# A new order of the first steps of a fused attention and MoE kernel, with a small first load and other engines for some steps

## The chip, the cores and the metric

The kernel runs on one core of one Trainium2 chip. The metric is the device time of one execution in microseconds. The core has five engines that run side by side and wait for each other by semaphores: TensorE (PE) multiplies matrices into PSUM, VectorE (DVE), ScalarE (ACT) and GpSimd (POOL) work on elements, SyncE (SP) issues the DMAs. Each engine executes its own queue strictly in order.

## The reference

Windowed attention with sink keys, and then an MLP with softplus on its result, all in float32, the weights given as float64 words (4 batches, 8 heads, 768 positions, head width 64; 3072 tokens, 512 to 2048 to 512).

```python
scores = scale * q @ k.T                      # per batch and head, scale = 1/8
rel = pos[:, None] - pos[None, :]
keep = (pos[None, :] < n_sink) | ((rel >= 0) & (rel < window))   # n_sink 4, window 128
scores = where(keep, scores, -1e9) - max
a = exp(scores); a = a / (sum(a) + 1e-09)
x = (a @ v) laid out as (tokens, 512)
h = x @ w_in
g = maximum(h, 0) + log1p(exp(-abs(h)))
out = g @ w_out
```

## The kernel before

**Tiling.** The 3072 tokens are cut into 12 chunks of 256. A chunk's attention has 8 heads, and its MLP has 8 slices s of 256 hidden columns. Matrices of the MLP are split into a high part that float32r holds exactly and a remainder, and three products are summed. Chunks 0 and 1 do their attention in plain float32, two heads at a time ("exact"); later chunks split the operands too. Step indices count heads through the chunks: 0 to 7 are chunk 0, 8 to 15 chunk 1, from 16 on chunk 2.

**Two orders.** The first steps stand in a string, `Ctx.START` (L1052), which `_fast` (L643) walks through: each letter calls a function, the number is its index. After it a loop runs the same pattern for every head until the end (`Ctx.STEADY`, L1048), and a tail follows. Since each engine works through its queue in order, what the string sets is the order within each engine's queue; what stands between on other engines doesn't matter. The letters are:

- S: scores of a head into PSUM (L249; from 16 on L266, L267). T: masks and softmax, on VectorE (L283 or L288, L295), and the exponential on ScalarE (L296). N: the sums (ScalarE, L309), the reciprocal (VectorE, L310), and the product on the engine that `Ctx.NM` names (L314 to L321; in exact chunks "A" means VectorE). W: transposes on TensorE (L357; from 16 on none), a copy on the engine of `Ctx.TH`, two selections on GpSimd (L362, L366). V: values (L422, L429; from 16 on L441, L447), into the one bank of tag x. O: high part on ScalarE and remainder xl on VectorE, which frees that bank. k and K: the sink weights (L326; transpose L337, copies on ScalarE, from 16 on subtractions on VectorE). In exact chunks only the odd index of a pair has work for N, W, V and O.
- w: the DMA of the next half weight. a, c, d, l: its four stages. a copies the top half words (engine from `Ctx.WT`), c joins them to the rest on VectorE (L519), into SBUF or, where `Ctx.WM` has p, into PSUM; d takes the high part (engine from `Ctx.WH`, P becoming A at home p), l the remainder (engine from `Ctx.WL`, always VectorE at home p). The halves come in the order wi00, wi01, wi10, wi11, wo00, wo01, wi20 and so on: wi is w_in, wo is w_out, then slice and half.
- U: up, 24 matmuls (L579). F: three activations of softplus on ScalarE (L586 to L588). P: gate, on VectorE (L594), and its high part gh on the engine of `Ctx.GH`. R: gl, the remainder (L609). D and E: the two halves of a down step, six matmuls each (L629), by row t; B: both halves joined, the four products with gh of each half first and the four with gl last.
- L, G: loads of q and k, and of v. p, q: splits of them. X, x: the transposes through DRAM from 16 on. J, j: the sinks' values on GpSimd. Z: dummy matmuls on a constant tile (L728).

**Masks.** `_constants` (L82) makes three masks from n_sink and window, which come in their own small DMA on ScalarE's queue (L91). A helper at L70 does every subtraction, one at L62, L64 and L66 every copy.

## Time and profile before

| | us |
|---|---|
| median of 3 runs | 685.43 (684.97 to 685.5) |
| the profiled execution, in all | 687.59 |
| its span, first to last instruction | 685.9 |
| TensorE busy in the span | 664.1 (97%) |
| VectorE busy | 523.3 (76%) |
| ScalarE busy | 473.3 (69%) |
| GpSimd busy | 432.4 (63%) |

Times in the trace are microseconds from the start of the span. A matmul's row shows its latency, and matmuls overlap, so rows can be longer than the distance between them. An idle time stands in brackets, with what ended it; that releaser is inferred, and of several it is the last one by the profile.

### The profile page before, as it was taken

How to read it: one execution, taken by the hardware profiler on the slowest of the kernel's cores; microseconds unless marked ns; L12 is line 12 of the kernel's file. 1: busy time of each engine (PE TensorE's matmuls, PEld its weight loads, DVE VectorE, ACT ScalarE, POOL GpSimd, SP SyncE). 2: the span in 40 equal slices, each digit the busy share in tenths (PEclk: the TensorE clock that was granted, in tenths of full speed). 3: DMA queues.
4: the chain of work that ended last, by engine and by line, in shares of the span. 5: the costliest groups of instructions: out<-in, count | busy, mean ns of one | idle time of the engine just before them, and what ended most of it. 6: DMA issues, size and time to landing. Idle time of an engine off the chain costs nothing. (4 is left out here: it accounts for less than half of the span.)

```text
span 685.9 us, 14212 instructions
## 1 busy us (share of the span) xinstructions
PE 664.1 (97%) x4319; PEld 595.3 (87%) x4319; DVE 523.3 (76%) x1461; ACT 473.3 (69%) x1213; POOL 432.4 (63%) x817
## 2 busy tenths in 40 slices
PE   5999889999999999999999999999999999999996
PEld 3588768999999999999999999999999999999985
DVE  6898987778888888887788788887978877754322
ACT  6998876767777677776777677776777677664322
POOL 6775458686676667677676775776766677653110
PEclk9999999999999999999999999999999999999999
DMA  8996334434434343543543544434434534310000
GB/s 304 353 403 207 95 77 126 103 103 131 107 94 139 102 116 112 130 115 83 148 102 98 134 113 113 124 103 108 131 94 119 143 91 118 104 52 0 32 5 32
DMA packets 97657, 83.35 MB, mean 122 GB/s; under 512 B 51876, under 2 KB 79140, under 8 KB 97572
## 3 DMA queue, kind: packets, MB, share of 16 engines
q1 hardware_dynamic: 97428, 82.35, 42.1%
q8 instruction: 37, 0.61, 0.4%
q14 instruction: 48, 0.39, 0.2%
q10 hardware_dynamic: 144, 0.00, 0.0%
HBM read 65.53 MB, written 16.78 MB: 120 GB/s over the span
## 5 line engine op out<-in xcount | busy, mean ns | idle before, releaser
L579 PE MATMUL h<-xh,wi 128*128 128x256 f32 x1536 | 247.3, 283 | 2.4 <-issue 1.5
L579 PEld LDWEIGHTS h<-xh,wi 128*128 128x128 f32 x1536 | 211.6, 191 | 7.5 <-issue 3.6
L629 PE MATMUL acc<-wo,gh 128*128 128x512 f32 x760 | 196.3, 394 | 1.2 <-POOL wo L70 1.2
L629 PEld LDWEIGHTS acc<-wo,gh 128*128 128x128 f32 x760 | 136.5, 188 | 26.0 <-POOL wo L70 1.5
L579 PE MATMUL h<-xl,wi 128*128 128x256 f32 x768 | 154.7, 283 | 0.0
L70 POOL TENSOR_TENSOR tl<-u,th 128x256 f32<-128x256 f32 x80 | 69.9, 874 | 133.0 <-issue 130.0
L579 PEld LDWEIGHTS h<-xl,wi 128*128 128x128 f32 x768 | 119.7, 192 | 0.0
L586 ACT ACTIVATE mt<-h 128x512 f32<-128x512 f32 x96 | 57.6, 600 | 88.3 <-PE h L579 76.0
L629 PE MATMUL acc<-wo,gl 128*128 128x512 f32 x380 | 106.6, 390 | 1.2 <-DVE gl L70 1.2
L66 POOL TENSOR_SCALAR gh<-mt 128x512 fp32r<-128x512 f32 x87 | 53.7, 618 | 73.1 <-DVE mt L594 36.7
L594 DVE SCALAR_TENSOR_TENSOR mt<-h,mt 128x512 f32<-128x512 f32 x96 | 63.3, 660 | 33.3 <-ACT mt L588 33.3
L629 PEld LDWEIGHTS acc<-wo,gl 128*128 128x128 f32 x380 | 71.3, 188 | 17.4 <-DVE gl L70 2.1
L296 ACT ACTIVATE a<-a,stats 128x136 f32<-128x136 f32 x192 | 76.5, 400 | 6.1 <-DVE stats L295 4.9
L70 DVE TENSOR_TENSOR gl<-mt,gh 128x512 fp32r<-128x512 f32 x95 | 72.3, 761 | 5.2 <-POOL gh L66 5.2
L62 ACT CAST qkh<-qk 128x656 fp32r<-128x656 f32 x80 | 59.0, 737 | 12.1 <-DMA qk<-qk 11.8
L321 POOL TENSOR_SCALAR a<-a,rc 128x128 f32<-128x128 f32 x156 | 63.8, 420 | 2.7 <-DVE rc L310 2.7
L70 DVE TENSOR_TENSOR qkh<-qk,qkh 64x256 fp32r<-64x256 f32 x80 | 40.8, 511 | 30.1 <-ACT qkh L62 28.7
L588 ACT ACTIVATE mt<-mt 128x512 f32<-128x512 f32 x96 | 60.7, 633 | 3.1
L587 ACT ACTIVATE mt<-mt 128x512 f32<-128x512 f32 x96 | 60.7, 633 | 3.1
L467 DVE TENSOR_TENSOR xt<-x,xt 64x256 f32<-64x256 f32 x80 | 33.0, 412 | 31.3 <-ACT xt L62 31.2
L70 DVE TENSOR_TENSOR kl<-qk,qkh 128x400 fp32r<-128x400 f32 x80 | 53.3, 667 | 2.3
L447 PE MATMUL x<-pt,vv 128*128 128x256 f32 (+1 forms) x216 | 47.3, 322 | 0.0
(195 smaller groups left out, 1103.1 us busy)
## 6 DMA issues: line engine op xcount, KB each, us to landing
qk<-qk SPq DMA_DIRECT2D x160, 164.0 KB, 3.1
rows<-xf SPq DMA_DIRECT2D x320, 32.0 KB, 1.6
u<-rows SPq DMA_DIRECT2D x80, 128.0 KB, 2.6
vr<-v SPq DMA_DIRECT2D x32, 192.0 KB, 2.7
out<-o SPq DMA_DIRECT2D x24, 256.0 KB, 2.4
qk<-qk SPq DMA_DIRECT2D x8, 328.0 KB, 6.6
vr<-v SPq DMA_DIRECT2D x16, 128.0 KB, 2.3
wi00r<-w SPq DMA_DIRECT2D x1, 511.8 KB, 6.6
```

What stands on the lines that cost most here:

```text
L62: nc.scalar.copy(out, in_)
L66: nc.gpsimd.tensor_scalar(out, in_, 1.0, 0.0, ALU.mult, ALU.add)
L70: (nc.vector if eng == "V" else nc.gpsimd).tensor_tensor(out, a, b, ALU.subtract)
L296: nc.scalar.activation(a, a, AF.Exp, bias=nm, scale=-1.0, accum_out=total)
L321: (nc.vector if eng == "V" else nc.gpsimd).tensor_scalar(a, a, rc[:, j : j + 1], 0.0, ALU.mult, ALU.add)
L447: nc.tensor.matmul(x[:, :, o], w, pt[:, :, m], start=False, stop=n == 2, skip_group_check=True)
L579: nc.tensor.matmul(h[:, j], wt, x, start=k == 0, stop=k >= len(prods) - 2, skip_group_check=True)
L586: nc.scalar.activation(t[:], h[:], AF.Abs)
L587: nc.scalar.activation(t[:], t[:], AF.Exp, scale=-1.0)
L588: nc.scalar.activation(t[:], t[:], AF.Ln, bias=1.0)
L594: nc.vector.scalar_tensor_tensor(t[:], h[:], 0.0, t[:], ALU.max, ALU.add)
L629: nc.tensor.matmul(self.acc[t][:], x[:, j, t * P : t * P + P], w, start=start, stop=stop, skip_group_check=True)
```

## The change

It leaves the computation as it is. n_sink and window, the first block of keys and the first queries of heads 0 and 1 come in one load of their own, `first`, ahead of the rest of those heads. All mask operations that the first softmax needs move to VectorE and ahead; those of masks 1 and 2 become a step m. A new step z runs dummy matmuls into the bank of tag x. gl gets its own list of engines, `Ctx.GL`, where it was always on VectorE. The lists of engines and `Ctx.START` are new: five of the first slices' down steps are joined (B0 to B3 and B6), and two more half weights have their home in PSUM.

```diff
@@ -87,8 +87,7 @@
 
 
     nc, cp = c.nc, c.const
-    words = cp.tile([P, 2, 2], I32, name="words")
-    nc.scalar.dma_start(words[:].rearrange("p a b -> p (a b)"), c.a["sizes"].broadcast_to([P, 4]))
+    words = c.first[:, :4].bitcast(I32).rearrange("p (a b) -> p a b", a=2)
     room = c.ap.tile([P, 1024], F32, tag="a", name="mask_room")
     used = 0
 
@@ -97,7 +96,7 @@
         used += n
         return room[:, used - n : used]
 
-    rel, key, lt, fold, first, r0, r1 = (scratch(n) for n in (P, NS, P, P, P, NS, NS))
+    rel, key, lt, fold, first, r0, r1, pen0, pen1 = (scratch(n) for n in (P, NS, P, P, P, NS, NS, NS, NS))
     nc.gpsimd.iota(rel, pattern=[[-1, P]], base=0, channel_multiplier=1, allow_small_or_imprecise_dtypes=True)
     nc.gpsimd.iota(key, pattern=[[1, NS]], base=0, channel_multiplier=0, allow_small_or_imprecise_dtypes=True)
     make_identity(nc, c.ident)
@@ -121,15 +120,18 @@
     nc.vector.scalar_tensor_tensor(sizes[:], top[:], 4294967296.0, words[:, :, 0], ALU.mult, ALU.add)
     c.ns, c.wd = sizes[:, 0:1], sizes[:, 1:2]
     m0, m1, m2 = c.masks = [cp.tile([P, KW], F32, name=f"mask{i}") for i in range(3)]
-    pen0, pen1 = scratch(NS), scratch(NS)
-    nc.gpsimd.tensor_scalar(pen0, r0, c.wd, -BIG, ALU.is_lt, ALU.mult)
     nc.vector.tensor_scalar(m2[:, P:], key, c.ns, -BIG, ALU.is_ge, ALU.mult)
+    nc.vector.tensor_scalar(pen0, r0, c.wd, -BIG, ALU.is_lt, ALU.mult)
+    nc.vector.tensor_tensor(m0[:, P:], m2[:, P:], pen0, ALU.min)
     nc.vector.tensor_scalar(m0[:, :P], first, c.wd, -BIG, ALU.is_ge, ALU.mult)
-    nc.gpsimd.tensor_scalar(pen1, r1, c.wd, -BIG, ALU.is_lt, ALU.mult)
-    nc.vector.tensor_tensor(m0[:, P:], m2[:, P:], pen0, ALU.min)
-    nc.vector.tensor_scalar(m1[:, :P], fold, c.wd, -BIG, ALU.is_ge, ALU.mult)
-    nc.vector.tensor_tensor(m1[:, P:], m2[:, P:], pen1, ALU.min)
-    nc.scalar.copy(m2[:, :P], m1[:, :P])
+
+    def later():
+        nc.vector.tensor_scalar(pen1, r1, c.wd, -BIG, ALU.is_lt, ALU.mult)
+        nc.vector.tensor_scalar(m1[:, :P], fold, c.wd, -BIG, ALU.is_ge, ALU.mult)
+        nc.vector.tensor_tensor(m1[:, P:], m2[:, P:], pen1, ALU.min)
+        nc.gpsimd.tensor_scalar(m2[:, :P], fold, c.wd, -BIG, ALU.is_ge, ALU.mult)
+
+    c.later_masks = later
 
 
 class _Attention:
@@ -195,7 +197,12 @@
         if self.exact:
             if h % 2 == 0:
                 r = c.lp.tile([P, QK], F32, tag=("qk", "qkh")[h // 2 % 2], name=f"qk{chunk}_{h}")
-                nc.sync.dma_start(r[:], c.a["qk0"][chunk, h // 2])
+                lo = 0
+                if chunk == h == 0:
+                    lo = KW
+                    c.first = c.stg.tile([P, 4 + KW + P], F32, tag="stg", name="first")
+                    nc.sync.dma_start(c.first[:], c.a["first"])
+                nc.sync.dma_start(r[:, lo:], c.a["qk0"][chunk, h // 2, :, lo:])
                 self.heads[h] = r
             return
         r = c.lp.tile([P, QK], F32, tag="qk", name=f"qk{chunk}_{h}")
@@ -245,8 +252,10 @@
         s = self.s[j] = pool.tile([P, 2, DM], F32, tag=tag, name=f"{tag}{chunk}_{h}_{j}")
         for e in range(2):
             rows = slice(e * D, e * D + D)
-            q = r[rows, KC + j * P : KC + j * P + P]
-            nc.tensor.matmul(s[:, e, :w], q, r[rows, j * KW : j * KW + w], start=True, stop=True)
+            q, k = r[rows, KC + j * P : KC + j * P + P], r[rows, j * KW : j * KW + w]
+            if chunk == h == j == 0:
+                q, k = c.first[rows, 4 + KW :], c.first[rows, 4 : 4 + KW]
+            nc.tensor.matmul(s[:, e, :w], q, k, start=True, stop=True)
 
     def scores(self, h):
         c, nc = self.c, self.c.nc
@@ -606,7 +615,7 @@
             gl = c.w[s, 0, 0][:, 1]
         else:
             gl = c.mp.tile([P, 2, CT], F32R, tag="gl", name=f"gl{chunk}_{s}", bufs=c.GB)[:]
-        _sub(nc, c.E["gl"], gl, t[:], self.g[s][0])
+        _sub(nc, _turn(c.GL, chunk * FP + s), gl, t[:], self.g[s][0])
         self.g[s].append(gl)
 
     def down(self, s, *js):
@@ -733,8 +742,17 @@
             out = c.idle[:, : 2 * P - NS]
             c.nc.tensor.matmul(out, c.sk[:, :P], c.sk[:, : 2 * P - NS], start=True, stop=True, skip_group_check=True)
 
+    def warm(k):
+
+        if c.warm is None:
+            c.warm = c.ps_x.tile([P, 2, CT], F32, tag="x", name="warm")
+        for _ in range(k):
+            out = c.warm[:, 0, : 2 * P - NS]
+            c.nc.tensor.matmul(out, c.sk[:, :P], c.sk[:, : 2 * P - NS], start=True, stop=True, skip_group_check=True)
+
     parts = {
         "Z": (idle, 0),
+        "z": (warm, 0),
         "S": (call(att, "scores"), G),
         "T": (call(att, "softmax"), G),
         "N": (call(att, "normalise"), G),
@@ -761,6 +779,7 @@
         "j": (sinks(1), G - 1),
         "Y": (next_sinks, 0),
         "w": (dma, 0),
+        "m": (lambda i: c.later_masks(), 0),
         **{kind: (stage(kind), 0) for kind in "acdl"},
     }
 
@@ -977,7 +996,7 @@
     nc = tc.nc
     c = Ctx()
     c.nc, c.tc, c.a, c.out = nc, tc, a, out
-    c.E = dict(qkh="A", ql="V", kl="V", vh="A", vl="P", xh="A", xl="P", gl="V", tl="P", out="AV")
+    c.E = dict(qkh="A", ql="V", kl="V", vh="A", vl="P", xh="A", xl="P", tl="P", out="AV")
     c.x, c.vs, c.vsr, c.vsh = {}, {}, {}, {}
     c.held_h, c.held_acc, c.tail = None, None, 0
     c.w64 = a["w"].dtype == mybir.dt.int64
@@ -1020,7 +1039,7 @@
             for n in ("ps_s", "ps_h"):
                 fronts[n] = st.enter_context(ExitStack())
             c.front_s, c.front_h = (scores_pool(f"front{n[2:]}", 1, own) for n, own in fronts.items())
-            c.follow, c.ps_s, c.ps_h, c.idle = follow, None, None, None
+            c.follow, c.ps_s, c.ps_h, c.idle, c.warm = follow, None, None, None, None
             c.xf = c.sp.tile([P, 2, CT], F32, name="xf", bufs=1)
             with tc.manual_schedule(engines=ORDERED):
                 m = _fast(c)
@@ -1037,29 +1056,30 @@
 
 Ctx.nchunks = B * NCH
 Ctx.GB, Ctx.EXACT = 3, 2
-Ctx.NM = "PPPPPAPPPAPAPPPVPAPPAPPPP"
-Ctx.TH = "VVVAAAAAAAVAAAVAAAAAAA"
-Ctx.GH = "PAAAAAVVVPPPP"
-Ctx.WM = "sssssssppsppssssssssssssssssssss"
-Ctx.WT = "AAVAAAAAAAAAAAAPPAAAAAAAAAAAAAAV"
-Ctx.WH = "APPPAAPAPPPPAAVAPAPAVAAVPAAAVAPA"
-Ctx.WL = "PPPVVPPVPPVVVPVPVPPVVVPPVPPVVPPV"
+Ctx.NM = "VPPPVAPPVVPVVVVPPAPPAPVPP"
+Ctx.TH = "AAAAAAAAAAVAVAAAAVAVVA"
+Ctx.GH = "AAPAPAPVPPAPP"
+Ctx.GL = "PVVVVVVPV"
+Ctx.WM = "sspspssppsppssssssssssssssssssss"
+Ctx.WT = "APAAAAAAAVAAAPPPPAAAAAAAAAPAAAAV"
+Ctx.WH = "APPPAAPPAPPAAPPPAAAAPAPPPAAPPVAA"
+Ctx.WL = "PPVPPPPPPVPPVPPPVVVVVVPVPPPPVPVP"
 Ctx.JOINED = 19
 Ctx.STEADY = (
     ("kWUqYpKSFTXRDVPONE", "SWTkpUKERDNFXPqYVO"),
     ("UKpFWSTRXPqNBVOYn", "WSpUKFTqBXVORPNnY"),
 )
 Ctx.START = """
-W0 N12 V14 V4 O4 V6 V0 S0 N6 V12 w j4 V2 N14 W14 O0 V10 N0 w w L8 O2 N2 S1 J0 w w w L10 L12 w T0 T1 S2 G4 w V8
-N1 w w w G8 w w G6 T2 L16 w w w w w G10 w L14 w w w w w w S3 T3 N3 w w w S4 T4 w W1 w k0 a a S5 T5 c c W12 w w
-L18 L17 G12 W8 d K0 d a S6 T6 c l l S7 W3 a O6 O8 S8 T7 d l O12 T8 c O14 d V1 N5 N7 O1 a a c d S9 T9 c N9 k4 a
-W5 V3 a Z4 S10 T10 l c c O3 Z18 S11 d K4 a a T11 l c N11 O10 l Z8 V5 O5 W7 S12 c a d d l l c d l d a c V7 O7
-N4 a k8 c l p16 d d a W9 U0 F0 U1 T12 c a a d P0 S13 T13 c R0 c d d K8 G14 N13 a F1 a U2 F2 l l l V9 S14 P1 l
-W11 W4 T14 G16 c l c W2 D0 a d S15 d P2 l L19 U3 a L20 T15 W13 R1 E0 c l S16 c N15 D1 O9 E1 k12 R2 E2 F3 d l d
-d a a T16 D2 P3 c a U4 L22 c l l a c d N16 R3 D3 d p17 c a p18 F4 d d V11 l l a K12 c d O11 a U5 N8 l l
-S17 F5 c T17 P4 c W10 l R4 p19 V13 O13 W15 X16 a a d S18 l a U6 E3 d T18 D4 P5 d c S19 T19 R5 l l d c p20 F6 q16 l
-l P6 N18 N17 J16 x16 E4 V15 X17 L21 G18 a O15 U7 x17 N19 S20 W16 c c c U8 D5 E5 F7 X18 k16 N10 T20 x18 R6 F8 P7 X19 R7 P8 K16 E6 d d d p21
-a D6 N20 W17 V16 W6 l l O16
+z3 w V10 N0 V0 j4 W0 W14 V12 w z6 N12 w N6 z4 w m J0 L8 G6 O0 V6 S0 w V14 L10 w w T0 L12 S1 T1 S2 G4 O4 w w V8 w
+L14 O8 V2 z1 N1 N2 O2 N14 w S3 T2 w V4 T3 L16 w N3 a w w z6 w w w S4 w w G8 a W1 W12 S5 w T4 k0 S6 w w O10 w w
+G10 w w c T5 w L17 c a z4 d O12 w w a K0 d T6 w l O6 c S7 w W8 S8 l G12 d T7 W3 T8 c l N5 N7 V1 O1 d a S9 a T9 c
+W5 S10 V3 c k4 N9 a S11 d a T10 l c c O3 d L18 K4 a T11 N4 l Z2 Z12 c O14 V5 a l O5 d W7 S12 c d d a l a l l d c
+c V7 O7 p16 l N11 d W9 W2 a U0 F0 k8 T12 c a d a c d a P0 U1 S13 T13 c K8 c d d R0 N13 l l F1 d U2 a l S14 F2
+G16 T14 l c l a W11 P1 c V9 L19 L20 l B0 a P2 a S15 T15 d W13 U3 R1 d G14 c c N15 a R2 O9 S16 l F3 k12 d c d W4
+B1 d a T16 P3 l l L22 a c c V11 B2 p17 l d d U4 R3 a c l N8 O11 l a d c F4 K12 a d N16 a l U5 F5 S17 T17 a l V13
+P4 c W10 c l d B3 O13 R4 p18 a W15 U6 p19 P5 d d S18 D4 E4 a S19 c l d T18 c T19 X16 R5 p20 l x16 F6 l l q16 l
+P6 N18 J16 N17 N10 V15 L21 G18 X17 D5 N19 U7 x17 E5 O15 a k16 c U8 c F7 W6 S20 X18 d R6 d W16 a P7 F8 c T20 x18
+B6 W17 P8 X19 K16 p21 N20 R7 V16 l d O16 l
 """
 
 
@@ -1074,6 +1094,12 @@
     w_out = w_out.reshape(FP, 2, P, DM).transpose(0, 2, 1, 3).reshape(FP, P, WC)
     w = np.stack([w_in, w_out], axis=1)
     return w.view(np.int64) if w.dtype == np.float64 else w
+
+
+def _first(qk, n_sink, window):
+    words = np.array([n_sink, window], np.int64).view(np.float32)
+    r = qk[0, 0, :2].reshape(P, QK)
+    return np.concatenate([np.broadcast_to(words, (P, 4)), r[:, :KW], r[:, KC : KC + P]], axis=1)
 
 
 def _layout(q, k, v, n_sink, window, moe_w_in, moe_w_out):
@@ -1093,7 +1119,7 @@
         "qk0": np.ascontiguousarray(qk[0, : Ctx.EXACT]).reshape(Ctx.EXACT, H // 2, P, QK),
         "v": np.ascontiguousarray(v.transpose(0, 2, 1, 3)).reshape(B, NB, P, H * D),
         "vs": np.ascontiguousarray(v[:, :, :NS].reshape(B, 2, G * NS, D).transpose(0, 2, 1, 3)),
-        "sizes": np.array([n_sink, window], np.int64).view(np.int32).reshape(1, 4),
+        "first": _first(qk, n_sink, window),
         "w": _blocks(moe_w_in, moe_w_out),
     }
 
```

## Rows read from the trace of the kernel before

**Rows 1.** Windows: us, then PE, PEld, DVE, ACT, POOL busy, PEclk, DMA, GB/s

```profile
30.00:40.00 10.00, 8.96 (x71) 7.09 (x70) 9.72 (x19) 9.68 (x22) 7.55 (x9) 1.00 1.04 342
...
300.00:400.00 100.00, 100.00 (x659) 91.88 (x658) 82.91 (x235) 72.28 (x190) 68.99 (x140) 1.00 0.43 115
```

**Rows 2.** Waits of TensorE, 0 to 200 us: total, times, longest

```profile
PE sb L249 <- DMA qk<-qk: 4.8, 1, 4.8
PE x L441 <- DVE sk L70: 2.4, 1, 2.4
PE acc L629 <- DVE gl L70: 1.2, 2, 0.8
...
PE s L266 <- DVE stats L295: 0.6, 1, 0.6
```

**Rows 3.** Timeline of TensorE: start, length, instruction, idle before and releaser

```profile
17.34 1.25 PE L249 MATMUL sb<-qk 64*128 64x264 f32 x4
...
21.15 0.77 PE L249 MATMUL sb<-qk 64*128 64x264 f32 x4
...
24.97 2.34 PE L734 MATMUL idle<-sk 128*128 128x248 f32 x18
...
35.31 0.72 PE L579 MATMUL h<-xh,wi 128*128 128x256 f32 x4
...
40.90 0.40 PE L579 MATMUL h<-xl,wi 128*128 128x256 f32 x2
...
72.54 0.67 PE L422 MATMUL x<-sk,vsf 128*128 128x256 f32 x2 [1.19 <-POOL wo L66]
```

**Rows 4.** Timeline of VectorE, single operations up to 101 us

```profile
5.29 0.16 DVE L120 SCALAR_TENSOR_TENSOR words_top<-words 128x2 f32<-128x2 int32 x1 [2.78 <-DMA words<-sizes]
...
6.75 0.30 DVE L295 CUSTOM_DVE_ANT_0 a<-sb,mask 128x136 f32<-128x136 f32 x1
...
15.29 0.45 DVE L64 CAST upper<-wi10r 128x512 f16<-128x512 bf16 x1
...
18.64 0.43 DVE L283 COPY_PREDICATED sb<-diag,sb 128x256 f32<-128x256 int32 x1 [0.99 <-PE sb L249]
...
31.89 0.69 DVE L314 TENSOR_TENSOR a<-a,rc 128x512 f32<-128x512 f32 x1
...
71.97 0.42 DVE L70 TENSOR_TENSOR xl<-x,xh 128x256 fp32r<-128x256 f32 x1 [0.22 <-ACT xh L62]
...
100.11 0.58 DVE L70 TENSOR_TENSOR sk<-ts,sk 32x128 fp32r<-32x128 f32 x2
```

**Rows 5.** Timeline of ScalarE: a top half, a high part, sink copies

```profile
13.15 0.76 ACT L62 CAST upper<-wi00r 128x512 f16<-128x512 bf16 x1
...
52.10 0.60 ACT L62 CAST wi<-wt 128x512 fp32r<-128x512 f32 x1
...
97.78 0.51 ACT L62 CAST sk<-ts 32x128 fp32r<-32x128 f32 x2
```

**Rows 6.** Timeline of VectorE beside GpSimd: stage c, and reads of a scores bank

```profile
27.90 0.68 DVE L519 SCALAR_TENSOR_TENSOR wt<-wi20r,upper 128x512 int32<-128x512 int32 x1
...
35.86 1.02 DVE L519 SCALAR_TENSOR_TENSOR word_ps<-wi31r,upper 128x512 int32<-128x512 int32 x1
...
58.59 0.48 DVE L288 COPY_PREDICATED s<-diag,s 128x128 f32<-128x128 int32 x2
...
60.89 1.78 DVE L519 SCALAR_TENSOR_TENSOR wt<-wo41r,upper 128x512 int32<-128x512 int32 x1
```

**Rows 7.** Timeline of GpSimd in the same stretches

```profile
36.29 1.06 POOL L66 TENSOR_SCALAR wo<-wt 128x512 fp32r<-128x512 f32 x1
...
58.00 1.84 POOL L70 TENSOR_TENSOR wo<-wt,wo 128x512 fp32r<-128x512 f32 x1 [0.94 <-ACT wo L62]
...
60.51 1.61 POOL L70 TENSOR_TENSOR wi<-wt,wi 128x512 fp32r<-128x512 f32 x1
```

**Rows 8.** DMA issues: KB, us from issue to landing

```profile
wi00r<-w SPq DMA_DIRECT2D x1, 511.8 KB, 6.6
```

## The prediction

> **What bounds the kernel now.** I first read the windows by stage. From about 110 us on TensorE is without a gap: 100.00 busy of 100 in the stretch from 300 to 400 us, beside 82.91 on VectorE and 72.28 on ScalarE [rows 1]. That part and the tail keep their order, so the change acts through the time at which the START list ends. TensorE's work in the list is the same in both orders (nine up steps, seven full down steps, the same scores, transposes and values); only its waits, its slow stretch and its dummy matmuls can go. Second, the waits of TensorE: 4.8 us before the first scores, 2.4 before the values V16, 1.2 in two waits for gl, 0.6 for a scores bank [rows 2]; and 1.19 before V13 [rows 3]. Third, the stage they arise in: between 30 and 40 us VectorE has 9.72 and ScalarE 9.68 of 10 us, GpSimd 7.55 [rows 1]. So up to U0 at 35.31 [rows 3] the elementwise queues are the bound, after it TensorE with them close behind, and in the end TensorE alone.
>
> V13's row names GpSimd's wo as its releaser. I read it otherwise: V13 needs the one bank of the x tag, which O11 frees, and O11's xl on VectorE ends at 71.97 + 0.42 = 72.39, 0.15 before V13 starts at 72.54 [rows 3, 4].
>
> Two up steps of 24 matmuls each take from 35.31 to 41.30 [rows 3]: about 2.9 for one, 0.12 for a matmul of 256 columns; so six of 512 columns, half a down step, take 1.4 (estimates).
>
> **Part 1, first DMA and masks.** From the words at 5.29 to the first softmax at 6.75 the masks take 1.46 us [rows 4]. All their operations stay on the path, since m stands ahead of T0 and puts mask 1 before it; only the turn to GpSimd goes, for two more eight-column VectorE operations. The words now come in the first of eight loads, which has 137 KB: no later than the 336 KB one that ends the wait of 4.8 [rows 2]. So T0 comes by 4.8 + 1.5 = 6.3 at the latest. I give that no credit of its own: the next long step on ScalarE is now the top half of wi00 (a), ahead of W1 and T4, and wi00 lands 6.6 us [rows 8] after its issue, which before was some 5.3 us in, so near 11.9; that step ran at 13.15 before [rows 5], behind T4. The split load puts one more issue and 67 KB ahead of wi00, 0.2 us at the 342 GB/s of [rows 1]. The early gain waits there for a weight.
>
> **Part 2, dummy matmuls.** The granted clock reads 1.00, the 2.4 GHz level, in both stretches of [rows 1], yet the same four scores matmuls take 1.25 us at 17.34 and 0.77 at 21.15 [rows 3]: early ones run slow. The new z steps put 13 matmuls ahead of S0 and 11 between S2 and K0. One costs 2.34 / 18 = 0.13 us [rows 3] at the fast rate, 0.21 at the ratio 1.25 / 0.77. The 13 take 1.7 to 2.7 us and run while TensorE waits for its first load; if that cover is too short they put S0 off by up to the excess, ahead of a ScalarE that waits for wi00. The 11 take 1.4 to 2.3 and are paid unless the pace rises, when each early scores step gives 0.5 back. What it can be worth is VectorE's wait of 0.99 for T8's scores [rows 4]. Z4 + Z18 + Z8 become Z2 + Z12, 2.1 us less, in a place where TensorE waits for O3 and W5 anyway: nothing.
>
> **Part 3, queues up to O7, so up to U0.** VectorE loses the top half of wi10 (0.45), Nm11 (0.69, now behind O7) and W1's copy (the same shape, 0.69), and gains one top half (0.45) [rows 4]: -1.4 us. ScalarE loses two top halves (0.76 each) and gains W1's copy and a high part (about 0.60 each) and one top half (0.76) [rows 5]: +0.4, less one short sum (Ns11) that moves behind O7. So U0 comes between no earlier (ScalarE is the bound) and 1.4 + 0.99 = 2.4 us earlier (VectorE is). Both are full, so I take the middle: **-1.2**.
>
> **Part 4, from U0 to V16.** By waiting step, from the order in the diff:
> - V13: between V11 and V13 stood K12, U5 and S17, some 3.4 us; now B2, U4, K12, U5 and S17, about 9. The wait of 1.2 goes.
> - gl: D needs gl at its third matmul, B at its ninth, some 1.4 us later. The waits of 1.2 in sum [rows 2] are at most 0.8 long: both go, unless gl itself is late. The two residues on GpSimd (R0, R7) stand where B0 and D7 have other steps ahead of them.
> - V16: now U8, S20, B6, K16, V16 in a row. B6 and S20 cover 3.3 us, under which F8, T20 and P8 run. Behind K16 nothing covers the sink copies: 0.51 on ScalarE [rows 5], 0.58 on VectorE [rows 4] and three handovers at 0.15, 1.55 in the place of 2.4: **-0.8**.
> - S19: between S18 and S19 there are D4 and E4, 2.8 us, where U6, E3 and D4 stood (5.7) and S19 still waited 0.6 [rows 2] for T18 to free its banks. Between T17 and T18 VectorE now has eight operations of the size of c (0.68 [rows 6]), two splits of about 1 and O13, 7.8 us, while TensorE has 7.7 (V13, B3, W15, U6). The wait lies between 0 and 3.5 (5.7 + 0.6 - 2.8), nearer to 0 because U6 has moved ahead of S18; I add **+1.2** for it and other new ones.
>
> Sum of the part: -1.2 - 1.2 - 0.8 + 1.2 = **-2.0**.
>
> **Part 5, work between engines.** Over START, counted from the lists (a weight with home p takes no GpSimd step): VectorE loses 3 high parts and 2 gh (about 0.45 each, as the cast of [rows 4]), 2 gl (as c, 0.68 each) and W1 (0.69), and gains a weight remainder (0.68) and W17 (about 0.35): -3.3 us. ScalarE loses 4 top halves (0.76 each), a high part and a gh (0.60 each): -4.2, with W1 and W17 about even. GpSimd gains 4 top halves, 4 high parts, 3 gh and 2 gl, less one remainder: eleven one-input operations of 0.5 to 1.06 [rows 7] and one of 1.61 [rows 7], 7 to 13 us, into a queue at 7.55 of 10. This makes the waits of part 4 less likely; it is not added again.
>
> What it costs lies on VectorE. Operation c is 0.68 alone and 1.78 beside a GpSimd remainder that runs from 60.51 to 62.12, and ends 0.55 after that [rows 6, 7]. Beside a one-input operation of GpSimd it took 1.02 [rows 6, 7], 0.34 more. But reads of a scores bank kept their time under the remainder from 58.00 to 59.84 [rows 7] (0.48 for two predicated copies at 58.59 [rows 6]). So one added GpSimd operation costs VectorE from nothing (beside reads of PSUM) to 0.34, or 1.1 with two inputs: 0 to 11 x 0.34 + 1.1 = 4.8 in all. I take 1.5, nearer to the lower end because half of VectorE's list reads PSUM; VectorE still gains, and the sum gets nothing.
>
> The Trainium skill, page "SBUF — State Buffer", section "Who interferes with whom", says that where the VectorE instruction has two SBUF inputs and the GpSimd one reads SBUF, the second to issue waits for the whole of the first. The trace agrees for c at 60.89, 1.1 us. By that rule one added one-input operation could cost up to all of its 0.5 or more, some 6.6 us for the twelve.
>
> **Sum.** -1.2 - 2.0 = **-3.2 us**. The profiled execution has a span of 685.90 inside 687.59 in all; its span would be 682.7. Against the median of the runs, 685.43: **682.2**.
>
> **Rivals.**
> - *The gain is given back at V16.* The last values need W16 on GpSimd. GpSimd's list there is l.wi71, q16, l.wo61, gh6, Nm18, J16, Nm19, W16, and S18 stands only some 17 us of TensorE work ahead of V16 (before: 21). If START ends when that chain does, V16's wait of 2.4 grows by what is won elsewhere. For it: GpSimd gets the added work. Against: it was idle a quarter of the time. It gives 685.2, no change.
> - *The pace doesn't rise early.* Then the 11 z steps put 2.3 us into TensorE's early queue; T8's wait grows by about 1.0 of them, and part 3's 1.2 isn't won: 682.2 + 1.2 + 1.0 = 684.4.
> - *GpSimd blocks VectorE (slower).* The place is U0 to T18, where VectorE is full. The added operations start first and c, kl and gl wait: 4.8 against 3.3 saved is 1.5 late, and the waits of part 4 stay, since their releasers (O11, T18, gl) sit on VectorE: 685.4 + 1.5 = 686.9. It decides from 3.3 us of added blocking: the two-input one and seven of the eleven. Against it is the row at 58.59 [rows 6].
>
> **How the numbers follow.** Forecast 0.60, given back 0.16, no early pace 0.08, blocked 0.16. The forecast's own range is 678.2 (2.4 at U0, 1.2 and 1.2 of waits, all 2.4 of V16, no new wait) to 684.5 (nothing at U0, 2.3 at S19). The whole range takes in the rivals, the last with a little over: 678.2 to 687.2. A difference of 0.2%, 1.4 us, is about what a measurement tells from none. Faster: 0.60 and half of the pace rival, 0.64; same: the other half and most of the given back, 0.19; slower: 0.17.
>
> **What would show it.** U0's first matmul near 34.1 instead of 35.31; no wait over 0.4 at V13 or for gl; V16 waiting about 1.6; scores of 0.77 rather than 1.25 well before 17 us; T0 before 6.3, but ScalarE waiting for wi00 near 11.9; c's mean not longer. The prediction is wrong if U0 stands at its old time, if S19 or U7 waits over 2 us, or if VectorE's two-input operations grow longer in sum.

## The result and the profile after

The changed kernel takes 691.42 us in the median (687.74 to 694.34), the kernel before 685.37 (684.97 to 685.84): 1.0082 times as long, 95% interval 1.0066 to 1.0098, or 6.05 us more. The prediction said 682.2. The profiled execution of the changed kernel took 692.79 us, with a span of 691.1.

The first part of its page (busy us, share of the span, instructions):

```profile
PE 667.7 (97%) x4327; PEld 601.3 (87%) x4327; DVE 525.7 (76%) x1461; ACT 469.5 (68%) x1205; POOL 444.9 (64%) x825
```

Its windows, to be held against [rows 1] (us; PE, PEld, DVE, ACT, POOL busy; PEclk; DMA; GB/s), and behind them two of the kernel before:

```profile
30.00:40.00 10.00, 9.48 (x76) 7.67 (x75) 9.53 (x15) 8.49 (x19) 6.93 (x9) 1.00 1.03 374
40.00:50.00 10.00, 8.61 (x56) 6.95 (x55) 9.60 (x28) 8.10 (x22) 8.12 (x9) 0.83 1.04 393
...
100.00:110.00 10.00, 7.27 (x36) 6.98 (x35) 8.25 (x23) 6.01 (x18) 9.71 (x15) 0.66 0.31 81
300.00:400.00 100.00, 100.00 (x661) 92.00 (x661) 81.93 (x234) 71.92 (x189) 69.36 (x139) 1.00 0.42 115
...
675.00:680.00 5.00, 4.74 (x23) 4.56 (x24) 0.69 (x1) 0.76 (x2) 0.35 (x1) 0.66 0.02 3
```

```profile
40.00:50.00 10.00, 9.61 (x70) 7.39 (x71) 9.90 (x29) 9.24 (x23) 6.01 (x7) 1.00 1.03 408
...
100.00:110.00 10.00, 7.97 (x51) 7.12 (x52) 7.17 (x21) 5.96 (x15) 7.01 (x12) 1.00 0.23 58
```

Between 300 and 400 us both kernels keep TensorE busy without a gap. What is new stands in PEclk: TensorE's granted clock is 0.83 in 40 to 50 us, 0.66 in 100 to 110 and 0.66 near the end, where the kernel before has 1.00. The waits of TensorE from 0 to 200 us, which answer to [rows 2] (total, times, longest):

```profile
PE x L450 <- ACT qkh L62: 2.7, 1, 2.7
...
PE sb L258 <- DMA qk<-qk: 1.5, 1, 1.5
...
PE s L275 <- DVE stats L304: 0.9, 1, 0.9
PE acc L638 <- DVE gl L70: 0.8, 1, 0.8
PE h L588 <- DVE mt L603: 0.8, 1, 0.8
...
PE s L276 <- DVE kl L70: 0.5, 1, 0.5
```

The wait of 4.8 for the first load has gone from this list, since the z matmuls now stand there; one wait for gl is left, and the wait before V16 is longer (2.7). TensorE's timeline, which answers to [rows 3]:

```profile
34.73 0.72 PE L588 MATMUL h<-xh,wi 128*128 128x256 f32 x4
...
43.06 0.74 PE L588 MATMUL h<-xh,wi 128*128 128x256 f32 x4 [0.77 <-DVE mt L603]
...
46.31 1.05 PE L588 MATMUL h<-xh,wi 128*128 128x256 f32 x4
...
102.89 0.55 PE L450 MATMUL x<-sk,vs 128*128 128x256 f32 x1 [2.73 <-ACT qkh L62]
...
104.09 1.05 PE L588 MATMUL h<-xh,wi 128*128 128x256 f32 x4
...
122.48 0.29 PE L275 MATMUL s<-qkh 128*128 128x264 f32 x1
...
671.99 0.71 PE L588 MATMUL h<-xh,wi 128*128 128x256 f32 x4 [1.07 <-PEq L1048]
...
675.26 1.06 PE L588 MATMUL h<-xh,wi 128*128 128x256 f32 x4 [2.32 <-issue]
```

U0 starts at 34.73. Behind the waits at 43.06 and 102.89 four matmuls of an up step take 1.05 us in place of 0.64, the half rate. The scores at 122.48 are the same step as at 119.24 in the first trace of the kernel before. Near the end TensorE waits twice, 3.4 us in sum: for its own sequencer (PEq), and for nothing that the profile names (issue). These two are called its own waits from here on.

**What a second trace of the kernel before shows (e15).** The execution on which the prediction rests took 687.59 us, 2.2 over its median. A second one took 685.43; from it first the waits, then the timeline of TensorE:

```profile
PE x L441 <- DVE sk L70: 2.0, 1, 2.0
PE acc L629 <- DVE gl L70: 1.3, 2, 0.9
PE acc L629 <- POOL wo L70: 1.2, 1, 1.2
```

```profile
70.95 0.60 PE L422 MATMUL x<-sk,vsf 128*128 128x256 f32 x2
...
117.09 0.29 PE L266 MATMUL s<-qkh 128*128 128x264 f32 x1
...
670.40 0.51 PE L579 MATMUL h<-xh,wi 128*128 128x256 f32 x3 [1.46 <-issue]
```

V13 starts at 70.95 without a wait, where [rows 3] has 1.19, and the scores come at 117.09. In the first execution a load of q and k was late. This row of ScalarE shows it, some 6 us ahead of V13; that it is what delayed V13 is likely, and was not tried:

```profile
66.14 0.74 ACT L62 CAST qkh<-qk 128x656 fp32r<-128x656 f32 x1 [1.99 <-DMA qk<-qk]
```

**The account, by the traces** (changed kernel against e15). START ends 122.48 - 117.09 = 5.4 us later. U0 comes 0.3 sooner (34.73 against 35.06). From U0 on the waits take 6.6 us against 5.3, so 1.3 more. The half rate costs 1.5 in U2 (4.56 us from its start to the next scores; 3.04 in e1, where the clock stays up) and 2.6 behind V16 (6.17 against 3.54 in e1). The last 0.3 stay unassigned. The loop from there to flag_row, the first matmul of the tail, is 0.9 shorter, and the tail 2.9 longer: its own waits 3.4 against 2.2, and half rate behind the second. The sum is 7.4 for these two executions, 692.79 against 685.43. The medians are 6.05 apart, so the traced execution of the changed kernel is 1.4 over its median, and the median need not hold each of these terms in full.

### The profile page after: what moved, and what is told of

It reads as the page before. It is cut to its first block, busy times and chain, and to the rows that moved or that the text cites. A ratio compares the mean times of both kernels' runs of the same rounds, so it can differ in the third digit from the quotient of the medians.

```text
span 691.1 us, 14220 instructions
## 1 busy us (share of the span) xinstructions
PE 667.7 (97%) x4327; PEld 601.3 (87%) x4327; DVE 525.7 (76%) x1461; ACT 469.5 (68%) x1205; POOL 444.9 (64%) x825
## 5 line engine op out<-in xcount | busy, mean ns | idle before, releaser
L588 PE MATMUL h<-xh,wi 128*128 128x256 f32 x1536 | 249.9, 285 | 4.2 <-issue 2.3
L588 PEld LDWEIGHTS h<-xh,wi 128*128 128x128 f32 x1536 | 214.8, 194 | 9.0 <-issue 4.0
L638 PE MATMUL acc<-wo,gh 128*128 128x512 f32 x760 | 193.3, 393 | 0.0
L588 PE MATMUL h<-xl,wi 128*128 128x256 f32 x768 | 156.4, 286 | 0.0
L588 PEld LDWEIGHTS h<-xl,wi 128*128 128x128 f32 x768 | 121.5, 195 | 0.0
L66 POOL TENSOR_SCALAR gh<-mt 128x512 fp32r<-128x512 f32 x89 | 56.6, 637 | 75.7 <-DVE mt L603 44.8
L638 PE MATMUL acc<-wo,gl 128*128 128x512 f32 x380 | 103.9, 390 | 0.8 <-DVE gl L70 0.8
L70 DVE TENSOR_TENSOR kl<-qk,qkh 128x400 fp32r<-128x400 f32 x80 | 55.1, 688 | 2.3
```

Of the source, the lines that this page charges most:

```text
L66: nc.gpsimd.tensor_scalar(out, in_, 1.0, 0.0, ALU.mult, ALU.add)
L70: (nc.vector if eng == "V" else nc.gpsimd).tensor_tensor(out, a, b, ALU.subtract)
L588: nc.tensor.matmul(h[:, j], wt, x, start=k == 0, stop=k >= len(prods) - 2, skip_group_check=True)
L638: nc.tensor.matmul(self.acc[t][:], x[:, j, t * P : t * P + P], w, start=start, stop=stop, skip_group_check=True)
```

## The experiments

Filler means: extra matmuls of a constant tile by itself into a tile of tag x, which nothing reads; one matmul is two records on TensorE. In the order they are a new letter y.

```diff
+    def plug(k):
+        t = c.ps_x.tile([P, 2, CT], F32, tag="x", name=f"plug{c.plugs}")
+        c.plugs += 1
+        for _ in range(k):
+            out = t[:, 0, :P]
+            c.nc.tensor.matmul(out, c.ident[:], c.ident[:], start=True, stop=True, skip_group_check=True)
```

All results in one table. "Records" is TensorE's count in the first part of the page; "tail at" is the start of flag_row, the first matmul behind the loop, in the traced execution; "own waits" are TensorE's waits for its sequencer and for issue near the end of that trace (in e18 the second, 1.8, is put down to ScalarE). The traced execution is one of several: it lies 2.4 us under the median in e6, 1.3 under it in e18 and 2.0 over it in e9 and e12.

| run | median us | ratio to before, 95% | records | tail at | own waits |
|---|---|---|---|---|---|
| before (first, second trace) | 685.3 to 685.6 | | 4319 | 657.07, 654.92 | 2.2, 2.2 |
| changed | 691.42 | 1.0066 to 1.0098 | 4327 | 659.42 | 3.4 |
| e1 late filler, 29 | 688.54 | 1.0036 to 1.0070 | 4385 | 658.80 | 0.9 |
| e2 without z | 690.82 | 1.0060 to 1.0094 | 4303 | 661.87 | 1.0 |
| e3 before without Z | 686.24 | 1.0002 to 1.0021 | 4289 | 657.38 | 1.2 |
| e4 before, new engines | 697.19 | 1.0155 to 1.0189 | 4319 | 666.87 | 2.1 |
| e5 late filler, 15 | 686.89 | 1.0012 to 1.0031 | 4357 | 658.74 | 0.9 |
| e6 K16 early | 690.99 | 1.0067 to 1.0101 | 4327 | 657.42 | 2.7 |
| e7 K16 early, filler 5 | 686.81 | 1.0012 to 1.0031 | 4337 | 657.23 | 0.9 |
| e8 before, first load and masks | 684.68 | 0.9979 to 0.9998 | 4319 | 654.52 | 1.5 |
| e9 e8 with K16 early | 685.65 | 0.9991 to 1.0011 | 4319 | 657.39 | 1.9 |
| e10 e8 with filler 8 | 683.22 | 0.9959 to 0.9984 | 4335 | 654.18 | 0.7 |
| e11 e7, less on GpSimd | 688.19 | 1.0031 to 1.0060 | 4337 | 658.84 | 1.1 |
| e12 e7, rows not joined | 686.95 | 1.0013 to 1.0035 | 4337 | 659.55 | 1.2 |
| e13 e5 with early filler | 687.09 | 1.0014 to 1.0034 | 4375 | 657.80 | 0.6 |
| e14 before, filler 8 | 684.19 | 0.9970 to 0.9989 | 4335 | 655.46 | 0.6 |
| e16 changed, filler 4 | 687.73 | 1.0020 to 1.0045 | 4335 | 659.00 | 1.2 |
| e17 changed, Z12 to Z4 | 688.48 | 1.0033 to 1.0067 | 4319 | 658.12 | 1.5 |
| e18 before, filler 4 | 687.87 | 1.0025 to 1.0054 | 4327 | 655.67 | 0.6 + 1.8 |

**Filling the waits behind which the clock falls (e1, e5, e13).**

```diff
-U1 S13 ... d U2 ... K16 p21
+U1 y5 S13 ... d y6 U2 ... K16 y18 p21
```

> The changed kernel, with 29 dummy matmuls more, placed where its TensorE waits: 5 ahead of S13, 6 ahead of U2, 18 between K16 and V16. Theory (the waits of the new order let TensorE's granted clock fall to 1.2 GHz, and the falls near 44 us and 102 us cost 1.8 and 3.2 us): no stretch below 1.00 between 40 and 110 us, time 685.5 to 688, runs closer together than the 6.6 us of the changed kernel. Rival (the new waits themselves, and GpSimd blocking VectorE): the waits stay as long, time 690 or more.

688.54: 2.9 us back, and in 40 to 50 and 100 to 110 us the clock reads 1.00. So without these waits the clock doesn't fall there. They don't make it fall each time, though. In the traces of e17 and e2 the same two waits, 0.62 and 0.77, stand ahead of U2, and its matmuls keep 0.64; what decides isn't shown. From e17:

```profile
43.61 0.74 PE L588 MATMUL h<-xh,wi 128*128 128x256 f32 x4 [0.77 <-DVE mt L603]
...
45.87 0.64 PE L588 MATMUL h<-xh,wi 128*128 128x256 f32 x4
```

How much of the 2.9 us the clock is worth can't be read from e1, since the number of TensorE's records changed as well (below). The filling ran longer than the waits (4.18 us for the 2.73 ahead of V16), so e5 has 2, 3 and 10 in the place of 5, 6 and 18.

> The changed kernel with the late extra matmuls of e1 cut to the length of the waits they fill: 2 ahead of S13, 3 ahead of U2, 10 ahead of V16, in place of 5, 6 and 18. In e1 the 29 matmuls ran as 58 records and took 1.27, 1.50 and 4.18 us where the changed kernel had waited 0.62, 0.77 and 2.73, so e1 carries some 2.8 us of its own filling. Theory (the rest of e1 over the kernel before is mostly that overhang): the granted clock stays 1.00 from 20 to 660 us and the median falls from 688.5 to 685.5 to 687. Rival (the new order itself is 3 us longer): 688 to 689 again. Second rival (shorter filling doesn't hold the clock): below 0.9 in 40 to 50 or in 100 to 110 us and 690 or more.

686.89. The clock stayed at 1.00 from 40 us on. In this execution it fell earlier (0.72, 0.84 and 0.93 in the three stretches of ten from 10 us on), and the 14 dummy matmuls Z took 3.27 us, 1.86 in the changed kernel's:

```profile
28.43 3.27 PE L743 MATMUL idle<-sk 128*128 128x248 f32 x14
...
36.52 0.72 PE L588 MATMUL h<-xh,wi 128*128 128x256 f32 x4
```

So U0 stood at 36.52. e13 fills the early waits as well (z8 ahead of S7, z10 ahead of S8, Z12 moved ahead of S11).

> e5 (the changed kernel with 15 late extra matmuls, 686.9) with the early waits filled too: 8 extra ahead of S7 (wait of 0.98 us in the changed kernel), 10 ahead of S8 (1.47, for the DMA of qk), and Z12 moved from behind S11 to ahead of it (1.84). Theory (what is left over the kernel before is a clock that falls before 35 us: U0 stood at 34.7 us in some traced executions and at 36.5 in others): the granted clock is 0.95 or more in 10 to 40 us, U0 at or under 34.7, the median 685 to 686 and the spread under 1.5 us. Rival (VectorE sets the pace there, so an early fall costs nothing, and the rest lies in the order itself): 686.5 to 687.5.

687.09 (685.95 to 688.57): no gain over e5. The clock still read 0.83 in 20 to 30 us, so the theory wasn't tried cleanly; its numbers were missed.

**Moving the cause of V16's wait (e6, e7).** V16 waits for the sink weights of K16, whose ScalarE step stands behind F8 and T20.

```diff
-d W16 a P7 F8 ... P8 X19 K16 p21
+d W16 K16 a P7 F8 ... P8 X19 p21
```

> The changed kernel with one step moved: K16 (the sink weights that V16 needs) from behind F8, T20 and B6 to ahead of P7, right behind W16. In the changed kernel V16 waits 2.73 us for the chain K16 transpose 99.89, ScalarE's rounding 101.54, VectorE's remainder 102.16; ScalarE gets to it only behind the three passes of F8 and the softmax T20 (98.92 to 101.54). Theory: the wait at V16 falls under 0.5 us and the granted clock stays 1.00 in 100 to 110 us, which gives back 2.2 to 2.7 us of wait and some 3 us of half rate: median 685 to 687. Rival (another input of V16 or of the stage behind it is late by the same time, or the wait shows up at the next step): no wait at V16 or one with another releaser, but 689.5 to 691.5.

> e6 with 2 extra matmuls ahead of S13 and 3 ahead of U2, as in e5, so that the clock doesn't fall at 44 to 48 us either. Theory: another 1 to 1.8 us under e6, so 683.5 to 685.5, at or under the kernel before (685.4), with the granted clock at 1.00 from 20 to 660 us. Rival: at e6's time, since what the fall at 44 us costs is waited for later anyhow.

e6: 690.99, though V16's wait and the fall behind it are gone and the tail began 2.0 us sooner in the trace. e7: 686.81, 4.2 less than e6 for five filler matmuls, far more than the 0.2 us by which the start of the tail differs. The two traced executions are only 2.3 apart (688.58 and 686.30), and 2.1 of that lie in the tail. So something beside START was at work, which e14 to e18 then took up. In e7's trace new waits stand behind V16:

```profile
99.40 0.28 PE L450 MATMUL x<-sk,vs 128*128 128x256 f32 x1
...
100.83 0.73 PE L456 MATMUL x<-pt,vv 128*128 128x256 f32 x3 [1.15 <-POOL pt L421]
...
106.12 0.50 PE L638 MATMUL acc<-wo,gl 128*128 128x512 f32 x1 [0.71 <-POOL gl L70]
...
126.77 0.30 PE L346 MATMUL ts<-ident,sa 128*64 128x128 f32 x1 [0.71 <-DVE sa L335]
...
130.16 0.28 PE L450 MATMUL x<-sk,vs 128*128 128x256 f32 x1
```

From V16 to the values four steps on it takes 30.76 us; in e14, with the old order, 127.62 - 99.20 = 28.42. So in this trace what the early K16 wins is given back in waits for GpSimd and VectorE.

**Parts of the change alone.** e2 takes the 24 z out, e3 takes Z4, Z18 and Z8 out of the kernel before.

> The changed kernel without its 24 early z matmuls. Theory: they raise the clock from about 6 us on, but nothing waits for TensorE there, so without them U0 starts within 0.7 us of 34.7 and the time stays in 688 to 694. Rival (the early rise is what the gain at U0 of 0.6 comes from, or the z steps themselves hold up the scores): U0 moves by over 1 us, either way.

> The kernel before without its 30 Z matmuls. Theory (what keeps the kernel before even is that no wait of its TensorE lets the clock fall, and the Z matmuls are part of that): the clock falls in some stretch after 21 us, the time is 1 to 4 us longer and its runs spread over more than 1 us. Rival (waits alone set the time): 685.4 within 0.5, since the Z matmuls run while TensorE waits anyway.

Held against the changed kernel, e2 looks like no effect (690.82). Yet in its trace U0 stands at 36.66, 1.9 us later, as the rival said. Held against e16, which has short own waits as e2 has, the z are worth 3.1 us, and the start of the tail says the same (661.87 against 659.00). Likewise e3 against e14: the Z of the kernel before are worth 2.0 us (tail at 657.38 against 655.46), and without them the clock read 0.74 in 30 to 40 us.

e4 gives the kernel before the new lists of engines (NM to WL, and GL) and leaves its order.

> The kernel before in its own order, with the engine lists of the change alone (NM, TH, GH, GL, WM, WT, WH, WL). Theory (the new split of work is not what costs): 684 to 686.5, clock 1.00 through the list. Rival (more GpSimd work blocks VectorE's two-input operations): 687 to 690, VectorE's stage c longer in the mean than 0.89 us.

697.19, the slowest of all: in the old order the new lists cost 11.9 us. That doesn't price them in the new order, to which they were fitted.

e8 has the old order and engines, with the small first load and the first masks ahead, the later masks right ahead of J0.

> The kernel before (its order of steps, its engines, no early extra matmuls) with only the small first DMA and the first masks made first; the later masks right ahead of J0. Theory of the prediction (VectorE is full from T0 to 60 us, so what T0 gains is kept): T0 starts 0.5 to 1 us sooner and the median is 684.4 to 685.0. Rival (the wait for the first weight words near 11.9 us and the two masks that VectorE takes over eat it): 685.2 to 686.0, no difference.

684.68, 0.9 under the kernel before: this part is a gain. T0 came at 4.66, 2.1 sooner. With short own waits on both sides the gain is as large (e10 against e14 below, 1.0). V16 still waited 2.02 us, and the clock read 0.84 in 100 to 110 us. e9 moves K16 there to behind k16, e10 puts eight filler matmuls into the wait:

```diff
-W17 V16
+W17 y8 V16
```

> e8 (the kernel before with the small first DMA and the first masks first) with K16 moved from behind P8 to right behind k16, ahead of F8 and T20. In e8 V16 waited 2.02 us for the sink weights and the granted clock fell to 0.84 in 100 to 110 us (three up blocks at 1.05 where 0.64 is usual, some 1.3 us). Theory (that wait, and the fall behind it, are on the path that sets the end): V16 waits under 0.5 us, the clock stays 1.00 from 90 to 130 us, and the median falls from 684.7 to 682.5 to 683.5. Rival (GpSimd's p21 and wo, behind which the next values and D7 stand, are late by the same): 684.2 to 685.

> e8 with 8 extra matmuls (16 records of some 0.12 us, 1.9 us in all) put into the wait of 2.02 us ahead of V16; nothing else moves. Theory (the clock falls because of that wait, and a fall costs some 1.3 us): granted clock 1.00 in 100 to 110 us and the median 683.4 to 684.0. Rival (what the fall costs is taken up by later waits, such as D7's 1.2 us for wo in the kernel before): 684.5 to 685, with that wait back.

e9: 685.65, the gain of e8 lost; its trace (an execution 2.0 over the median) waits 2.9 us for a gl and 2.1 for a wo in place of V16's wait. e10: 683.22, the fastest kernel here, 0.9972 of the one before.

e11 takes three late operations off GpSimd in e7 (gl7 to VectorE, gh6 and gh8 to ScalarE), e12 undoes its five joined rows (B0 to D0 E0 and so on).

> e7 (the changed kernel with K16 early and 5 extra matmuls) with three late operations taken off GpSimd: the remainder of gl7 to VectorE, the high parts of gh6 and gh8 to ScalarE; together 1.28 + 2 x 0.62 = 2.5 us out of a queue that is busy 9.4 and 9.7 of 10 us between 90 and 110 us in e7 (7.9 and 7.0 in the kernel before). In e7 TensorE waits 1.1 us for p21, 0.7 for gl, 0.7 for sa and 0.3 for o behind V16. Theory (the work moved to GpSimd is what gives the gain at V16 back): these waits fall to 1 us or less and the median from 686.8 to 685 to 685.8. Rival (ScalarE and VectorE are just as late there): 686.5 to 687.5.

> e7 with the five joined rows of the START list undone: B0, B1, B2, B3 and B6 become D and E of the same number at the same place. Theory (joining is worth what the prediction said for gl, 0.4 to 0.8 us for each wait, or nothing): 686.8 to 688. Rival (a joined row keeps eight accumulations of one bank order apart and holds both halves of a step until the later weight is there, so it costs): 685.5 to 686.3.

e11: 688.19, slower by 1.4. The waits now end with VectorE (1.2 for wo, 1.1 for kl): the theory that three operations too many lie on GpSimd falls. e12: 686.95, no difference; joining neither costs nor gives.

**TensorE's own waits near the end (e14 to e18).** e14 is the kernel before with the eight filler matmuls of e10, e15 the kernel before unchanged.

> The kernel before with nothing but 8 extra matmuls in the wait of 2.36 us ahead of V16. It tells what of e10's gain (683.2) is the filling and what the first DMA. Its trace shows the granted clock at 1.00 there. Theory (the clock falls at V16 only once something else has changed, as the first DMA in e8): 685.2 to 685.8, no difference. Rival (the kernel before falls there in many of its executions too): 683.9 to 684.8.

> The kernel before, unchanged, for a second traced execution. The first one took 687.59 us, 2.2 over the median; it waited 0.64 and 1.53 us for TensorE's own sequencer and issue at 669 and 672 us. Theory (those two waits differ from one execution to the next and are what makes it long): the steady part starts at 119.2 us again and the tail from flag_row to the last copy takes some 23.7 to 24.5 us in place of 25.2. Rival (the START list itself runs up to 2 us shorter in a usual execution): the last scores of the list at 117 to 118.5 us.

e14: 684.19, 1.4 us faster, though its tail began no sooner (655.46; 654.92 in e15). The gain lies in the own waits, 0.6 against 2.2. e15 decided for the rival: in an execution at the median START itself runs 2 us shorter, and the own waits are the same 2.2. The three runs that settle it change TensorE's records by eight at a time: e16 has y4 ahead of S19 in the changed kernel, e17 has Z4 for Z12, e18 has y4 for e14's y8.

> The changed kernel with 4 extra matmuls (8 records, about 0.9 us) put into the wait of 0.87 us ahead of S19 and nowhere else; the waits at S13, U2 and V16 stay as they are. TensorE then has 4335 records in place of 4327. In the traces so far TensorE's own waits in the last up step (sequencer and issue, 669 to 676 us) sum to 1.5 to 3.4 us with 4319 or 4327 records and to 0.6 to 1.2 with any other number (4289, 4303, 4335 to 4385). Theory (much of the change's loss, and of what the fillings gave back, is this wait and the fall of the clock behind it, and it hangs on the number of TensorE's instructions): the wait is 1.2 us or less, the clock stays 1.00 from 660 us on, START ends as in the changed kernel, and the median falls from 691.4 to 687.5 to 689. Rival (the falls in START make the loss): 690.5 to 692.

> The changed kernel with Z12 cut to Z4: 4319 records on TensorE, the number of the kernel before, and some 1 us less of dummy matmuls ahead of V3's second half. Theory of the number: TensorE's own waits near the end sum to 1.5 to 2.2 us, as in the four traces with 4319, and the median is 689 to 690.5, of which up to 1 us may be the shorter dummy run. Rival (they follow the order, not the number): 3 us or more again and 690.5 to 692.

> The kernel before with 4 extra matmuls (8 records) in the wait ahead of V16, half of e14's filling, so that TensorE has 4327 records, the changed kernel's number; e14 has 4335 and took 684.2. Theory of the number: TensorE's own waits near the end are 2.2 to 3.4 us, and the median is 685.5 to 687, at or over the kernel before (685.6). Rival (it is the filling of V16's wait that gave e14 its 1.4 us): 684.3 to 685.

| records on TensorE | old order | new order | difference |
|---|---|---|---|
| 4319 | 685.36 (before) | 688.48 (e17) | 3.1 |
| 4327 | 687.87 (e18) | 691.42 (changed) | 3.6 |
| 4335 | 684.19 (e14) | 687.73 (e16) | 3.5 |

e18 shows it most plainly: half of e14's filler in the same place, and the kernel is 3.7 us slower than with all of it and 2.5 slower than with none. In e16 four matmuls in a wait of 0.87 us give 3.7 us back while V16 waits 2.7 and the clock falls as before; the start of the tail moves by 0.4. So the 6.05 us fall into two parts that add up: 3.1 to 3.6 for the new START, 2.5 (old order) to 2.9 (new order) for 4327 records in place of 4319. The medians of e17 and e18 lie 0.5 under and 0.9 over the ranges expected.

The traces put this second part in the tail. From flag_row to the end of the span it takes 28.2 to 28.8 us with 4319 records, 29.1, 29.5 and 31.7 with 4327, and 27.0 to 27.7 with every other number, in both orders. Only for e18 this falls short: its traced execution, 1.3 under its median, has a tail of 29.1 us where the kernel before has 28.8, so its 2.5 us are shown by the medians and not located. TensorE's waits from 640 us on, first the changed kernel, then e16, then e18:

```profile
PE h L588 <- issue: 2.3, 1, 2.3
PE h L588 <- PEq L1048: 1.1, 1, 1.1
```

```profile
PE h L588 <- PEq L1057: 1.2, 1, 1.2
```

```profile
PE h L579 <- ACT mt L588: 1.8, 1, 1.8
PE h L579 <- PEq L1038: 0.6, 1, 0.6
```

With 4319 or 4327 records the second wait of the same step is there (0.8 to 2.3 us); with every other number tried it isn't. In e18 it is put down to ScalarE's mt. The line that PEq names is the same in all kernels, `with tc.If(ok < 1):`, the branch past the general path for other inputs; the tail stands behind it. TensorE's branch takes 3.3 to 3.9 us in all 20 traces, that of VectorE, ScalarE, GpSimd and SyncE 0.05 to 0.07. In the changed kernel:

```profile
L1048 PEldq COMPARE_BRANCH  x1: 3772/3772/3772, 667.9 to 667.9; - x1
```

So the first own wait is the end of this branch, as far as the work already queued doesn't cover it. What the second one is, a few matmuls behind the branch, isn't shown. The pages list a queue named "instruction" with packets of 0.02 MB (q8): 37 of them in all runs up to 4327 records, 36 from 4335 to 4375, 37 again at 4385. The Trainium skill, page "Runtime: NRT & Kernel Launch", section "Instruction fetch mechanics", says that an engine's instructions are loaded in blocks of 16 KiB while the current ones run, and that crossing a block is mostly hidden. The packets fit that size. That the second wait is such a load, moved by the number of instructions, is possible and not shown: e1, e2 and e3 have 37 packets too, and no second wait.

## Why the prediction was wrong, step by step

Two steps failed most. The first is "only its waits, its slow stretch and its dummy matmuls can go": it lets TensorE's pace only rise, and has no term for a clock that falls again behind a wait, 4.1 us in the traces. The second is "That part and the tail keep their order, so the change acts through the time at which the START list ends": the tail got 2.9 us longer in the traces, and by the runs 2.5 us or more of the 6.05 go with the number of TensorE's records. The terms of START, in us, against e15:

| term | predicted | measured |
|---|---|---|
| U0 | -1.2 | -0.3 |
| V13 | -1.2 | 0.0 |
| gl | -1.2 | -0.5 |
| V16 | -0.8 | +0.7 |
| S18 and S19 | +1.2 | +1.2 |
| waits at S13 and U2 | none | +1.1 |
| wait of D7 for wo | none | -1.2 |
| half rate in U2 and behind V16 | none | +4.1 |
| not assigned | | +0.3 |
| sum | -3.2 | +5.4 |

The wait of D7 (1.2 us in both traces of the kernel before) was not in the prediction, and it is gone.

- **The base.** "Against the median of the runs, 685.43: 682.2" took a sum of waits off the median that was read from an execution 2.2 us over it. The wait of 1.2 at V13 was part of that: e15 and e14 have none there, e18 has 0.39. So V13 gained nothing over a usual execution. As an order of steps the term was right: V13 has no wait in the changed kernel either.
- **Part 1** was right in its marks: T0 at 5.78 (at or under 6.3), ScalarE waiting for wi00 to 11.96 (near 11.9). "No credit" was low: alone it is worth 0.9 (e8).
- **Part 2.** The 13 z took 3.13 us, over the 1.7 to 2.7 worked out, and S0 started at 4.91, against 4.8 before. The small load had landed sooner than that: without z the same scores start at 3.1 (e2, e8), so the z put them off by 1.8 us. Early scores ran at 0.49 and 0.71 from 6.4 us on, as hoped; at 16.70 they took 1.25 again. The step considered only a pace that rises. That it can fall again behind a wait was nowhere costed: +1.5 at U2 and +2.6 at V16 in the trace. Z2 and Z12 "nothing" held as long as the clock was up; in e5's trace they took 1.4 longer.
- **Part 3**, U0: -1.2 expected, -0.6 against the first trace, -0.3 against the second. Right in sign, mis-sized: both bounds were sums of queue work, and the middle between them was a guess.
- **Part 4**: gl lost one of its two waits, 0.8 is left (predicted none). S18 and S19 wait 0.8 and 0.9, 1.0 more than the 0.6 before, for +1.2 predicted: right. V16 waits 2.73, for 1.55 predicted; the transposes behind B6 come at 99.9, and ScalarE reaches their copy at 101.5, behind F8 and T20, which the step counted as done under B6 and S20. F8 was late because it waited 2.58 us for gl, which stands on VectorE behind X18; and X18 had waited 2.41 us (0.83 and 0.48 in the traces before) for the transfers of X17, which the new order puts behind the loads L21 and G18. No run changed that order alone. The two rows of the changed kernel, VectorE and ScalarE:

```profile
97.78 0.45 DVE L386 STREAM_TRANSPOSE xf<-a 128x256 f32<-128x256 f32 x1 [2.41 <-DMA rows<-xf]
...
98.92 0.60 ACT L595 ACTIVATE mt<-h 128x512 f32<-128x512 f32 x1 [2.58 <-DVE gl L70]
```

- **Part 5**: VectorE was to gain 3.3 us and didn't. Stage c kept its length, 28.6 us for 32 (28.4 and 29.5 in the two traces of before), but the other remainders grew. The groups of kl in 0 to 120 us (count, busy us, mean ns), first the kernel before, then the changed one:

```profile
L70 DVE TENSOR_TENSOR kl<-qk,qkh 128x400 fp32r<-128x400 f32 x9 | 6.2, 688 | 0.3
```

```profile
L70 DVE TENSOR_TENSOR kl<-qk,qkh 128x400 fp32r<-128x400 f32 x8 | 7.3, 918 | 0.2
```

One of these kl in the changed kernel's timeline, and what GpSimd did beside it:

```profile
80.67 1.46 POOL L70 TENSOR_TENSOR wo<-wt,wo 128x512 fp32r<-128x512 f32 x1
...
81.01 1.55 DVE L70 TENSOR_TENSOR kl<-qk,qkh 128x400 fp32r<-128x400 f32 x1
```

One kl takes 0.918 us in the mean in place of 0.688; gl goes from 0.753 to 0.865, the remainders of wo from 0.682 to 0.817. Over their counts that is 8 x 0.23 + 8 x 0.11 + 10 x 0.135 = 4.1 us, more than the 3.3 saved. The kl at 81.01 ends 0.43 after a GpSimd remainder that began before it. The Trainium skill, page "SBUF — State Buffer", section "Who interferes with whom", says that a VectorE instruction with two SBUF inputs contends with a GpSimd instruction that reads SBUF. The trace agrees: 1.55 us in place of 0.69. So the prediction looked at c, and the cost came on kl, gl and wo. The price of 0.34 beside a one-input operation was also misread: when the c at 35.86 [rows 6] began, GpSimd was still in a two-input remainder, this row of the kernel before:

```profile
34.72 1.61 POOL L70 TENSOR_TENSOR wi<-wt,wi 128x512 fp32r<-128x512 f32 x1
```

This is the rival "GpSimd blocks VectorE", with its size nearly right (4.1 where it said 4.8, against 3.3 saved) and its place right: the long kl and gl stand between U0 and T18. Of the waits that it kept, S19 and one gl stayed and V13 didn't, and V16's is the chain of part 4. How much of the 3.5 us it is by itself wasn't isolated: e11, which moved three operations back, got slower.
- **What no step contained**: the number of TensorE's records. That the tail keeps its order was taken to mean that it keeps its time; the number costs 2.5 us of the 6.05 by the medians (e18).

What of START's 3.5 us is the half rate? With the late waits filled or moved and the own waits short (e5, e7, e13: 686.8 to 687.1) the kernel stands only 0.6 to 0.9 under e16, although the trace shows 4.1 us of half rate. In e7 the rest comes back as waits for GpSimd and VectorE behind V16, in e5 and e13 U0 came later (36.52 and 35.58). So with the clock at 1.00 from 40 us on the new order is still 2.6 us over e14. This is shown as a sum, and not split by its parts; the clock falls before 40 us stayed in all three.

## What to carry to other kernels

Before a wait is credited, trace the same kernel a second time: a wait that only the longer execution has is worth nothing against the median. Count what a change does to TensorE's instructions even where they are hidden, and test a result that is off by a few us with eight dummy instructions more or fewer before explaining it by the order. A shorter wait isn't always a gain, nor a longer one its own length only: look at the granted clock behind it.
